# Joint tiles of the first batch placed ahead of the second batch's last conv unit and projection, with 25 seven-product groups in place of 21

## The chip, the cores and the metric

The kernel runs on one core of one Trainium2 chip. The metric is the device time of one execution in microseconds (us). The engines are named as the profile names them: PE is TensorE (the matrix engine), DVE is VectorE, ACT is ScalarE, POOL is GpSimd and SP is SyncE, which issues most transfers here.

## The reference

Two strided convolutions with gelu, a projection, and the joint network of a speech transducer. All inputs are bfloat16; B = 2, T = 4000, D = 512, K = 5 taps, U = 8.

```python
h = sum over i of xp[:, i:i+T, :] @ w1[i];   h = gelu(h)[:, ::2, :]      # 2000 rows a batch
f = sum over i of hp[:, i:i+T1, :] @ w2[i];  f = gelu(f)[:, ::2, :]      # 1000 rows a batch
fe = jnp.einsum("btd,de->bte", f, w_f)
ge = jnp.einsum("bud,de->bue", g, w_g)
j = jnp.tanh(fe[:, :, None, :] + ge[:, None, :, :])
return jnp.einsum("btud,dv->btuv", j, w_o)                               # (2, 1000, 8, 512)
```

The joint part is the largest: j has 2 x 8 x 1000 = 16000 rows of 512, each multiplied by the 512 x 512 matrix w_o.

## The kernel before

**Conv stages.** The first convolution is done in five tiles (a fast-filter form on TensorE, with combinations of inputs and weights made by DVE and ACT). The second, conv2, is computed with a form that yields three outputs per step: `Triple.unit(m, ...)` handles one batch b and one block m of 128 output channels. A unit consists of a first part (five products of four matmuls of 334 columns, then an ACT copy `cs` and five DVE scalar steps into `sd` and `acc`, and one gelu into `fT`) and of an end (four more products, t0, s0, ti and si, and two gelus), which is put on a list and emitted by `finish` one or two units later. `conv2(b, m)` in the changed kernel is the body of the old double loop. `fe(b)` is the projection by w_f: eight groups of four matmuls of 500 columns, half of them copied to `feT` by DVE and half by ACT.

**Joint stage.** The 16000 rows make 125 tiles of 128. `tanh(v, k)` is one ACT instruction: 128 channels (k of 4) of the 1000 rows of one (b, u) pair v (16 pairs), from feT[b] with a bias from ge, into `jT`, a ring of 3072 columns (split in two where the ring wraps). `tanhs(upto)` issues those that are needed up to a column, and a few ahead where the ring has room. A tile goes one of two ways:

- `Plain`: four matmuls of 512 columns into one bank of PSUM, one DVE eviction into `ost`, one store.
- `Seven`: four tiles at once as a 2 x 2 block product with seven multiplications instead of eight (Strassen's in Winograd's form). A product is four matmuls of 256 columns. `sums()` makes four combinations `ss` of jT: three on POOL, one on DVE (number 2). `wosums()` makes those of w_o, `tw`, once. The products accumulate in PSUM and are read out on the way: p1 is kept by ACT in an fp32 buffer `sn` (s1), p6 adds to the same bank and is kept (u2), p5 has its own bank and is kept (d5), and p2, p3 and p7 are each followed by a DVE add of a bank and a kept buffer into `og`, p4 by a plain eviction (DVE, or ACT in every fourth group). p3 adds to p5's bank, p7 and p4 to p1's, so each of p6, p3, p7 and p4 waits until the bank has been read. Four tiles are then stored from og.

Before, there are 21 groups and 41 plain tiles. The loop body for group q, with p the one before it and r its two plain tiles, is: p1(q), p7(p), p5(q), p2(q), first plain tile, sums of the next group, p6(q), p4(p), p3(q), second plain tile. fe(1) stands in the first iteration, behind p2.

**What sets the order.** Every operation is recorded with what it reads and writes, a cost and its place. From the point where `pl.pin = False`, a planner (`schedule`) lists operations onto the engines by estimated times: DVE and ACT take, of what is ready, the one with the least slack; TensorE, POOL and SP take the earliest recorded. The result is one static list per engine, with semaphore waits for what crosses engines. An engine works its list in order: an instruction that waits holds up all behind it.

Of the kernel before, what the change touches and what calls it, by code (L numbers as in the profile page):

```python
# [10 lines left out]
FP16 = mybir.dt.float16  # L11
FP32 = mybir.dt.float32
P = 128
# [260 lines left out]
def bass_standalone__seq2seq_rnn_t_joint__speech_kernel(  # L274
# [19 lines left out]
    B, T, D = x.shape  # L294
    K = w1.shape[0]
    U = g.shape[1]
    NK = D // P
    assert (B, T, D, K, U) == (2, 4000, 512, 5, 8)
    T1, T2 = T // 2, T // 4
# [5 lines left out]
    RING = 3072  # L305
    BU = B * U
    NT = 512
# [3 lines left out]
    with ExitStack() as es:  # L311
        cur = [16512]

        def at(name, shape, dtype, offset=None):
            o = cur[0] if offset is None else offset
            b = Buf(nc, name, shape, dtype, o)
            if offset is None:
                cur[0] = (b.end + 31) // 32 * 32
            return b

        xs = [at(f"xs{i}", [4, NK, XW], BF16) for i in range(3)]
# [3 lines left out]
        xt_off = cur[0]  # L325
        xt = [at(f"xt{i}", [4, NK, NT], BF16) for i in range(2)]
# [5 lines left out]
        hT = [at(f"hT{b}", [6, NK, HWID], BF16) for b in range(B)]  # L332
# [3 lines left out]
        ty = [at(f"ty{i}", [2, 256], FP32) for i in range(3)]  # L336
# [14 lines left out]
        assert row[0].bytes <= xt[0].bytes  # L351
        jT = at("jT", [NK, RING], BF16, w1_off)
        fT = [at("fT0", [NK, T2], BF16, jT.end), at("fT1", [NK, T2], BF16, xt_off)]
        feT = [at(f"feT{b}", [NK, T2], FP32, xs[2 * b].end - xs[2 * b].bytes) for b in range(B)]
        og = [at(f"og{i}", [4, NT], BF16, h_off + i * 4096) for i in range(3)]
        ost = [at(f"ost{i}", [NT], BF16, h_off + 12288 + i * 1024) for i in range(3)]
        assert fT[0].end <= xt_off and ost[-1].end <= h_off + hT[0].bytes
        h1 = hT[1].end - hT[1].bytes
        sn = [at(f"sn{i}", [NT], FP32, h1 + i * 2048) for i in range(7)]
        assert sn[-1].end <= hT[1].end  # L360
        ss = [at(f"ss{i}", [4, 2, NT // 2], FP16, xs[1].end - xs[1].bytes + i * 4096) for i in range(4)]
        assert ss[-1].end <= xs[1].end
        tw = at("tw", [4, 2, NT // 2], FP16, wg_sb.end - wg_sb.bytes)
        assert tw.end <= wg_sb.end
        ps = Psum(es.enter_context(nc.psum_tensor("acc", [P, 8 * NT], FP32)))
# [4 lines left out]
        def vec_cost(o, ins, fast=True):  # L370
            bf = fast and all(not v.psum and v.ap.dtype == BF16 for v in (o,) + tuple(ins))
            return o.ap.free_size() * (0.52e-3 if bf else 1.04e-3) + 0.065
# [3 lines left out]

        def tt(eng, o, a, b, op):
            pl.op(eng, lambda e: e.tensor_tensor(out=o.ap, in0=a.ap, in1=b.ap, op=op), (a, b), (o,),  # L378
                  0.15 + 2.2e-3 * o.ap.free_size() if eng == "pool" else vec_cost(o, (a, b)))

        def act(o, i, func, scale=1.0, bias=None):
            rd = (i,) if bias is None else (i, bias)
# [176 lines left out]
        def finish(keep=0):  # L559
            while len(ends) > keep:  # L560
                ends.pop(0)()
# [300 lines left out]
        def fe(b):  # L862
            for half in range(2):
                for m in range(NK):
                    v = ps.cols(bank(), NP2)
                    sl = slice(half * NP2, (half + 1) * NP2)
                    mm(v, [(wf_sb[k, m * P:(m + 1) * P], fT[b][k, sl]) for k in range(NK)], True, True)
                    o = feT[b][m, sl]
                    if m % 2:
                        act(o, v, ACT.Copy)  # L870
                    else:
                        pl.op("dve", lambda e, o=o, v=v: e.tensor_copy(out=o.ap, in_=v.ap), (v,), (o,), vec_cost(o, (v,)))  # L872

        def tanh(v, k):

            b, u = v // U, v % U
            lo, hi = v * T2, (v + 1) * T2
            while lo < hi:
                n = min(hi - lo, RING - lo % RING)
                t = lo - v * T2  # L880
                act(jT[k, lo % RING:lo % RING + n], feT[b][k, t:t + n], ACT.Tanh,
                    bias=geT[k * BU + v:k * BU + v + 1])
                lo += n
# [9 lines left out]
        def tail_zero(b):  # L893
            v = hT[b][2:6, :, HOFF + NT3 - 1:HOFF + NT3]
            memset(v)
# [9 lines left out]
        for qi in range(1, len(tiles)):  # L905
            tile = tiles[qi]
            nx = tiles[qi + 1] if qi + 1 < len(tiles) else None
            for m in range(WHOLE if qi == 1 else 0, NK):
# [12 lines left out]
                    tail_zero(0)  # L921
                if qi == 4 and m == 1:
                    ge()
        for b in range(B):
            for m in range(NK):
                steps, mid = LATE[b, m], ()
                if (b, m) == (0, 0):
                    mid = [lambda: finish(1), lambda: tail_zero(1)]
                if (b, m) == (1, 1):
                    mid = [lambda: fe(0)]  # L930
                trip[b].unit(m, [lambda b=b, w=w: trip[b].step(w) for b, w in steps], mid)
                if b == 1 and m in (2, 3):
                    for k in (2 * m - 4, 2 * m - 3):
                        tanh(0, k)


        ntile = B * U * T2 // P
        sems = {}
# [50 lines left out]
        class Seven:  # L989
# [4 lines left out]
            def __init__(self, jt):  # L994
                self.jt, self.n = jt, Seven.count
                Seven.count += 1
                self.c = jt * P % RING
                assert self.c + NT <= RING
                self.S = ss[self.n % len(ss)]
                self.o = og[self.n % len(og)]  # L1000

            def a(self, r, k):
                return jT[2 * k:2 * k + 2, self.c + r * H:self.c + (r + 1) * H]

            def sums(self):
                S = self.S
# [5 lines left out]

            def product(self, i, bk, start, check=False):

                lhs = {1: lambda t, k: jT[k, self.c + t * P:self.c + (t + 1) * P],
                       2: lambda t, k: jT[2 + k, self.c + t * P:self.c + (t + 1) * P],
                       4: lambda t, k: jT[2 + k, self.c + H + t * P:self.c + H + (t + 1) * P]}.get(i)
                if lhs is None:
                    si = {5: 0, 6: 1, 7: 2, 3: 3}[i]
                    lhs = lambda t, k: self.S[si, k, t * P:(t + 1) * P]  # L1020
                rhs = {1: lambda k: wo_sb[k, 0:H], 2: lambda k: wo_sb[2 + k, 0:H], 3: lambda k: wo_sb[2 + k, H:NT]}.get(i)
                if rhs is None:
                    ti = {5: 0, 6: 1, 7: 2, 4: 3}[i]
                    rhs = lambda k: tw[ti, k]
                for t in range(2):
                    mm(ps.cols(bk * NT + t * H, H), [(lhs(t, k), rhs(k)) for k in range(2)], start and t == 0, True, False)
# [29 lines left out]
            def p5(self):  # L1056
                self.D = take()
                self.product(5, self.D, True)
                self.d5 = self.keep("act", self.D)

            def p2(self):
                bk = take()
# [26 lines left out]
        def tanhs(upto, spread=None):  # L1089

            while state[0] < B * U and not pend and state[0] * T2 < upto + 900:
                pend.extend((state[0], k) for k in range(NK))
                state[0] += 1
            while pend and (pend[0][0] * T2 < upto or spread):
                v = pend[0][0]
                fits = (v + 1) * T2 - RING <= state[1] or (v + 1) * T2 <= RING
                if v * T2 >= upto and not fits:
                    break
                assert fits
                tanh(*pend.pop(0))  # L1100
                spread = None
                if not pend and state[0] < B * U and state[0] * T2 < upto:
                    pend.extend((state[0], k) for k in range(NK))
                    state[0] += 1

        plain = [Plain(0), Plain(1)]
        seven = [Seven(2 + 6 * i) for i in range(20)] + [Seven(121)]
        rest = [[Plain(6 * i + 6), Plain(6 * i + 7)] for i in range(18)] + [[Plain(n)] for n in (114, 115, 120)]
        wosums()
        tanhs(2 * P)  # L1110
        plain[0].go()
        plain[1].go()
        finish()
        tanhs(seven[0].jt * P + NT)
        seven[0].sums()
        for i, (q, r) in enumerate(zip(seven, rest)):
            p = seven[i - 1] if i else None
            state[1] = (p or q).jt * P
            base = q.jt * P
            if i + 1 < len(seven):  # L1120
                tanhs(seven[i + 1].jt * P + NT)
            else:
                tanhs(ntile * P)
            q.p1()
            if p:
                p.p7()
            q.p5()
            q.p2()
            if i == 0:
                fe(1)  # L1130
            if i + 1 < len(seven):
                r[0].go()
            if i + 1 < len(seven):
                seven[i + 1].sums()
            tanhs(base, True)
            q.p6()
            if p:
                p.p4()
            q.p3()
            if len(r) == 2:  # L1140
                r[1].go()
        seven[-1].p7()
        rest[-1][0].go(True)
        seven[-1].p4(True)

        pl.emit(block, [(s[0], s[1]) for s in sems.values()])

# [27 lines left out]
```

## Time and profile before

| | us |
|---|---|
| three timed runs | 265.88, 304.03, 1554.93 (median 304.03) |
| profiled execution | 265.86 |
| its span, first to last instruction | 264.1 |
| TensorE busy, granted clock | 257.3, 1.00 |
| DVE, ACT, POOL busy | 209.9, 196.2, 80.1 |
| first joint product (p1 of group 0) starts | 154.82 |
| last matmul starts | 259.73 |
| DMA, mean over the span | 121 GB/s |

The costliest groups of the joint stage (from 134 us on), in the profile's form: the line and engine, out<-in, count, busy time and the mean of one.

| group | count | busy us | mean ns |
|---|---|---|---|
| ACT jT<-feT,geT 128x1000 (the uncut tanh) | 44 | 50.2 | 1198 |
| DVE og<-acc,sn 128x512 | 63 | 42.3 | 684 |
| ACT sn<-acc 128x512 | 63 | 39.6 | 677 |
| DVE ost<-acc 128x512 | 40 | 27.3 | 682 |
| POOL ss, three kinds | 63 | 73.6 | 1164 to 1180 |
| DVE ss<-jT 128x512 | 21 | 16.7 | 797 |
| DVE og<-acc (p4's eviction) | 15 | 10.3 | 685 |

A duration counts from start to end of one instruction. Instructions of one engine overlap (the next starts before the last one's result is out), so the rate is read from the distance of two starts. A line of the timeline such as "188.86 1.46 PE ... x8" gives the start, the length and how many instructions were merged into it; "[0.18 <-PE acc]" behind a line is the idle time before it and what ended that.

### The profile page before, as it was taken

The page shows a single profiled execution, that of the slowest core. Times are in us where ns is not written, and L with a number is a line of the kernel's source. Part 1 is how long each engine was busy: PE and PEld are TensorE (multiplying, and loading weights), DVE is VectorE, ACT ScalarE, POOL GpSimd, SP SyncE. Part 2 cuts the span into 40 slices and gives each one's busy share as a digit, 9 for nine tenths or more (in the row PEclk, how much of TensorE's full clock was granted, in tenths as well). Part 3 has the DMA queues.
Part 4 walks back from the last instruction along what each step waited for, and adds up shares of the span by engine and source line. Part 5 has one row for each costly group of instructions (what it writes and reads, how often), then busy time and mean ns, then how long its engine had stood idle before and what let it go on. Part 6 is the DMA issues. An engine that isn't in the chain of part 4 may idle for free.

```text
span 264.1 us, 4770 instructions
## 1 busy us (share of the span) xinstructions
PE 257.3 (97%) x1738; PEld 167.3 (63%) x1738; DVE 209.9 (79%) x320; ACT 196.2 (74%) x269; POOL 80.1 (30%) x85
## 2 busy tenths in 40 slices
PE   8899999999999999999999999999999999999993
PEld 4797954444444445566646665777777777777782
DVE  1898999929999996299663744789899899889993
ACT  2637989348348723685679993898999999999942
POOL 1000000000000710000000974055785886929760
PEclk9999999999999999999999999999999999999999
DMA  6999999997000000000000000354454554645555
GB/s 246 301 178 196 201 211 217 191 352 224 2 0 0 0 2 0 0 2 1 0 2 0 20 24 0 126 167 159 155 185 142 170 180 139 207 144 171 168 181 172
DMA packets 54725, 31.92 MB, mean 121 GB/s; under 512 B 31646, under 2 KB 54446, under 8 KB 54702
## 3 DMA queue, kind: packets, MB, share of 16 engines
q1 hardware_dynamic: 54558, 31.55, 44.6%
q8 instruction: 14, 0.23, 0.4%
q14 instruction: 9, 0.07, 0.1%
q10 hardware_dynamic: 144, 0.07, 0.1%
HBM read 7.86 MB, written 16.38 MB: 92 GB/s over the span
## 4 chain that ended last, share of the span: by engine, by line
PE 88%; ACT 8%; DVE 1%; issue 1%; ACTq 0%
PE acc L391 88%; ACT jT L383 4%; ACT fT L383 2%; DVE xs L466 0%; ACT cs L383 0%; ACT xt L383 0%; ACT feT L383 0%; DVE xt L378 0%; DVE feT L872 0%; ACT og L383 0%; ACT hT L383 0%; PE acc L459 0%; ACTq L965 0%; ACT ost L383 0%; DVE zero L398 0%
## 5 line engine op out<-in xcount | busy, mean ns | idle before, releaser
L383 ACT ACTIVATE jT<-feT,geT 128x1000 bf16<-128x1000 f32 (+10 forms) x84 | 78.4, 1012 | 2.4 <-PE acc L391 1.4
L391 PE MATMUL acc<-wo_sb,jT 128*128 128x512 bf16 (+1 forms) x336 | 61.3, 323 | 0.0
L378 DVE TENSOR_TENSOR og<-acc,sn 128x512 bf16<-128x512 f32 x63 | 42.3, 684 | 9.9 <-ACT sn L383 7.4
L391 PE MATMUL acc<-xt,w_sb 128*128 128x252 bf16 (+2 forms) x240 | 45.9, 333 | 0.3 <-ACT hT L383 0.3
L378 POOL TENSOR_TENSOR ss<-jT 128x512 f16<-128x512 bf16 x21 | 24.4, 1164 | 71.5 <-PE acc L391 49.5
L391 PEld LDWEIGHTS acc<-wo_sb,jT 128*128 128x128 bf16 x336 | 32.9, 98 | 16.5
L383 ACT ACTIVATE sn<-acc 128x512 f32<-128x512 f32 x63 | 39.6, 677 | 4.3 <-PE acc L391 4.1
L391 PE MATMUL acc<-tw,ss 128*128 128x256 f16 x252 | 34.7, 273 | 0.0
L391 PEld LDWEIGHTS acc<-xt,w_sb 128*128 128x128 bf16 x240 | 23.3, 98 | 17.9 <-DVE ty L533 0.5
L955 DVE CAST ost<-acc 128x512 bf16<-128x512 f32 (+1 forms) x41 | 27.7, 676 | 2.4 <-PE acc L391 2.1
L391 PE MATMUL acc<-xs,w_t 128*128 128x498 bf16 (+2 forms) x140 | 29.5, 341 | 0.0
L391 PEld LDWEIGHTS acc<-tw,ss 128*128 128x128 f16 x252 | 24.6, 98 | 7.2
L383 ACT ACTIVATE hT<-acc 128x996 bf16<-128x996 f32 (+2 forms) x13 | 12.6, 968 | 21.0 <-PE acc L391 21.0
L378 POOL TENSOR_TENSOR ss<-jT,ss 128x512 f16<-128x512 bf16 x21 | 24.7, 1180 | 0.7
L378 POOL TENSOR_TENSOR ss<-ss,jT 128x512 f16<-128x512 f16 x21 | 24.5, 1169 | 0.7
L383 ACT ACTIVATE xt<-xs 128x1992 bf16<-128x1992 bf16 (+2 forms) x14 | 21.6, 1576 | 2.6 <-DMA xs<-in_x_dram 2.6
L391 PEld LDWEIGHTS acc<-xs,w_t 128*128 128x128 bf16 x140 | 13.5, 98 | 10.9 <-issue 0.3
L391 PE MATMUL acc<-xs,w_sb 128*128 128x252 bf16 (+2 forms) x104 | 19.3, 318 | 1.2 <-DVE xt L378 1.2
L378 DVE TENSOR_TENSOR ss<-jT 128x512 f16<-128x512 bf16 x21 | 16.7, 797 | 4.2 <-PE acc L391 2.2
L378 DVE TENSOR_TENSOR xt<-xt,xs 128x1992 bf16<-128x1992 bf16 (+2 forms) x14 | 14.2, 1012 | 5.7 <-ACT xt L383 5.7
L533 DVE SCALAR_TENSOR_TENSOR sd<-acc,cs 128x334 f32<-128x334 f32 x16 | 7.4, 499 | 12.9 <-PE acc L391 12.4
L391 PE MATMUL acc<-row,w_sb 128*128 128x334 bf16 x96 | 17.5, 305 | 0.0
(71 smaller groups left out, 363.3 us busy)
## 6 DMA issues: line engine op xcount, KB each, us to landing
out_dram<-og SPq DMA_DIRECT2D x75, 128.0 KB, 2.0
w_sb<-in_w_dram SPq DMA_DIRECT2D x10, 512.0 KB, 5.6
out_dram<-ost SPq DMA_DIRECT2D x34, 128.0 KB, 2.0
xr<-in_x_dram SPq DMA_DIRECT2D x2, 512.0 KB, 3.6
wg_sb<-in_w_g_dram SPq DMA_DIRECT2D x1, 512.0 KB, 8.8
wf_sb<-in_w_f_dram SPq DMA_DIRECT2D x1, 512.0 KB, 7.0
wo_sb<-in_w_o_dram SPq DMA_DIRECT2D x1, 512.0 KB, 7.9
xs<-in_x_dram SPq DMA_TRANSPOSE x16, 5.6
```

The source lines that it names most:

```text
L378: pl.op(eng, lambda e: e.tensor_tensor(out=o.ap, in0=a.ap, in1=b.ap, op=op), (a, b), (o,), 0.15 + 2.2e-3 * o.ap.free_size() if eng == "poo ...
L383: pl.op("act", lambda e: e.activation(o.ap, i.ap, func, scale=scale, bias=0.0 if bias is None else bias.ap), rd, (o,), o.ap.free_size() * ...
L391: ins = e.matmul(o.ap, lhsT=l.ap, rhs=r.ap, start=start and n == 0, stop=stop and n == len(pairs) - 1, skip_group_check=not check)
L533: pl.op(eng, lambda e: e.scalar_tensor_tensor(out=o.ap, in0=a.ap, scalar=f, in1=b.ap, op0=ALU.mult, op1=add), (a, b), (o,), vec_cost(o, (a ...
L955: pl.op("dve", lambda e: e.tensor_copy(out=o.ap, in_=v.ap), (v,), (o,), vec_cost(o, (v,)))
```

## The change

The diff, with lines that only move buffers' assertions cut:

```diff
-        feT = [at(f"feT{b}", [NK, T2], FP32, xs[2 * b].end - xs[2 * b].bytes) for b in range(B)]
+        feT = [at("feT0", [NK, T2], FP32, xs[0].end - xs[0].bytes), at("feT1", [NK, T2], FP32, xt[1].end - xt[1].bytes)]
...
-        h1 = hT[1].end - hT[1].bytes
-        sn = [at(f"sn{i}", [NT], FP32, h1 + i * 2048) for i in range(7)]
-        ss = [at(f"ss{i}", [4, 2, NT // 2], FP16, xs[1].end - xs[1].bytes + i * 4096) for i in range(4)]
+        homes = [xt_off + 8192 + i * 2048 for i in range(4)] + [y.end - y.bytes for y in ty]
+        sn = [at(f"sn{i}", [NT], FP32, o) for i, o in enumerate(homes)]
+        ss = [at(f"ss{i}", [4, 2, NT // 2], FP16, xs[2].end - xs[2].bytes + i * 4096) for i in range(4)]
...
-                  0.15 + 2.2e-3 * o.ap.free_size() if eng == "pool" else vec_cost(o, (a, b)))
+                  0.02 + 2.14e-3 * o.ap.free_size() if eng == "pool" else vec_cost(o, (a, b)))
...
-        for b in range(B):
-            for m in range(NK):
...
-                trip[b].unit(m, [lambda b=b, w=w: trip[b].step(w) for b, w in steps], mid)
-                if b == 1 and m in (2, 3):
-                    for k in (2 * m - 4, 2 * m - 3):
-                        tanh(0, k)
+        def conv2(b, m):
...
+            trip[b].unit(m, [lambda b=b, w=w: trip[b].step(w) for b, w in steps], mid)
+
+        for m in range(NK):
+            conv2(0, m)
+        for m in range(2):
+            conv2(1, m)
...
-                self.c = jt * P % RING
+                self.c = [(jt + 2 * r) * P % RING for r in range(2)]
...
-                self.d5 = self.keep("act", self.D)
+                self.d5 = self.keep("dve" if self.n < 15 else "act", self.D)
...
-        plain = [Plain(0), Plain(1)]
-        seven = [Seven(2 + 6 * i) for i in range(20)] + [Seven(121)]
-        rest = [[Plain(6 * i + 6), Plain(6 * i + 7)] for i in range(18)] + [[Plain(n)] for n in (114, 115, 120)]
+        seven = [Seven(2 + 4 * i) for i in range(15)] + [Seven(62 + 6 * i) for i in range(10)]
+        rest = [[] for _ in range(15)] + [[Plain(66 + 6 * i), Plain(67 + 6 * i)] for i in range(10)]
+        hooks = {4: lambda: conv2(1, 3), 5: finish, 9: lambda: fe(1)}
         wosums()
-        tanhs(2 * P)
-        plain[0].go()
-        plain[1].go()
+        for k in range(NK):
+            tanh(0, k)
+        conv2(1, 2)
         finish()
-        tanhs(seven[0].jt * P + NT)
+        Plain(0).go()
+        Plain(1).go()
...
-            if i == 0:
-                fe(1)
...
+            if i in hooks:
+                hooks[i]()
         seven[-1].p7()
-        rest[-1][0].go(True)
+        Plain(122).go()
         seven[-1].p4(True)
+        Plain(123).go()
+        Plain(124).go(True)
```

In words: the groups become 25 and the plain tiles 25. Groups 0 to 14 cover tiles 2 to 61 (almost all of the first batch's 62.5) with no plain tile between them; groups 15 to 24 have two plain tiles each, as before; tiles 122 to 124 are plain and come last. The second batch's conv2 units 0 and 1 stay ahead of the joint stage, unit 2 is recorded after the first four tanh, unit 3 behind group 4, its end behind group 5, and fe(1) behind group 9. The keeping of d5 goes from ACT to DVE in groups 0 to 14. A group's four tiles may now lie across the ring's end (two pairs with addresses of their own). sn, ss and feT1 lie in other memory: sn over the end of xt0 and the three ty, ss over xs2, feT1 over xt1. The planner's cost for a POOL operation on 512 columns falls from 1.28 to 1.12.

More of the change, by code (lines that the diff above doesn't have):

```diff
@@ L353, in bass_standalone__seq2seq_rnn_t_joint__speech_kernel @@
         fT = [at("fT0", [NK, T2], BF16, jT.end), at("fT1", [NK, T2], BF16, xt_off)]
-        feT = [at(f"feT{b}", [NK, T2], FP32, xs[2 * b].end - xs[2 * b].bytes) for b in range(B)]
+        feT = [at("feT0", [NK, T2], FP32, xs[0].end - xs[0].bytes), at("feT1", [NK, T2], FP32, xt[1].end - xt[1].bytes)]
+        assert feT[1].end <= xt[1].end and fT[1].end <= xt_off + 8192
         og = [at(f"og{i}", [4, NT], BF16, h_off + i * 4096) for i in range(3)]
@@ L357, in bass_standalone__seq2seq_rnn_t_joint__speech_kernel @@
         assert fT[0].end <= xt_off and ost[-1].end <= h_off + hT[0].bytes
-        h1 = hT[1].end - hT[1].bytes
-        sn = [at(f"sn{i}", [NT], FP32, h1 + i * 2048) for i in range(7)]
-        assert sn[-1].end <= hT[1].end
-        ss = [at(f"ss{i}", [4, 2, NT // 2], FP16, xs[1].end - xs[1].bytes + i * 4096) for i in range(4)]
-        assert ss[-1].end <= xs[1].end
+        homes = [xt_off + 8192 + i * 2048 for i in range(4)] + [y.end - y.bytes for y in ty]
+        sn = [at(f"sn{i}", [NT], FP32, o) for i, o in enumerate(homes)]
+        assert sn[3].end <= xt[0].end
+        ss = [at(f"ss{i}", [4, 2, NT // 2], FP16, xs[2].end - xs[2].bytes + i * 4096) for i in range(4)]
+        assert ss[-1].end <= xs[2].end
         tw = at("tw", [4, 2, NT // 2], FP16, wg_sb.end - wg_sb.bytes)
@@ L923, in bass_standalone__seq2seq_rnn_t_joint__speech_kernel @@
                     ge()
-        for b in range(B):
-            for m in range(NK):
[L926 to L930, printed above, removed]
-                trip[b].unit(m, [lambda b=b, w=w: trip[b].step(w) for b, w in steps], mid)
-                if b == 1 and m in (2, 3):
-                    for k in (2 * m - 4, 2 * m - 3):
-                        tanh(0, k)
+        def conv2(b, m):
+            steps, mid = LATE[b, m], ()
+            if (b, m) == (0, 0):
+                mid = [lambda: finish(1), lambda: tail_zero(1)]
+            if (b, m) == (1, 1):
+                mid = [lambda: fe(0)]
+            trip[b].unit(m, [lambda b=b, w=w: trip[b].step(w) for b, w in steps], mid)
[3 more added lines that the diff above has]
+            conv2(1, m)
         ntile = B * U * T2 // P
@@ L996, in __init__ @@
                 Seven.count += 1
-                self.c = jt * P % RING
-                assert self.c + NT <= RING
+                assert jt % 2 == 0 and RING % (2 * P) == 0
+                self.c = [(jt + 2 * r) * P % RING for r in range(2)]
                 self.S = ss[self.n % len(ss)]
@@ L1002, in a @@
             def a(self, r, k):
-                return jT[2 * k:2 * k + 2, self.c + r * H:self.c + (r + 1) * H]
+                return jT[2 * k:2 * k + 2, self.c[r]:self.c[r] + H]
             def sums(self):
@@ L1013, in product @@
             def product(self, i, bk, start, check=False):
-                lhs = {1: lambda t, k: jT[k, self.c + t * P:self.c + (t + 1) * P],
-                       2: lambda t, k: jT[2 + k, self.c + t * P:self.c + (t + 1) * P],
-                       4: lambda t, k: jT[2 + k, self.c + H + t * P:self.c + H + (t + 1) * P]}.get(i)
+                tile = lambda r, t, k: jT[k, self.c[r] + t * P:self.c[r] + (t + 1) * P]
+                lhs = {1: lambda t, k: tile(0, t, k), 2: lambda t, k: tile(0, t, 2 + k),
+                       4: lambda t, k: tile(1, t, 2 + k)}.get(i)
                 if lhs is None:
@@ L1119, in bass_standalone__seq2seq_rnn_t_joint__speech_kernel @@
             base = q.jt * P
[L1120 to L1123, printed above, removed]
+            last = i + 1 == len(seven)
+            tanhs(ntile * P if last else seven[i + 1].jt * P + NT)
             q.p1()
@@ L1128, in bass_standalone__seq2seq_rnn_t_joint__speech_kernel @@
             q.p2()
-            if i == 0:
-                fe(1)
-            if i + 1 < len(seven):
+            if r:
                 r[0].go()
-            if i + 1 < len(seven):
+            if not last:
                 seven[i + 1].sums()
@@ L1139, in bass_standalone__seq2seq_rnn_t_joint__speech_kernel @@
             q.p3()
-            if len(r) == 2:
+            if r:
                 r[1].go()
+            if i in hooks:
+                hooks[i]()
         seven[-1].p7()
-        rest[-1][0].go(True)
+        Plain(122).go()
         seven[-1].p4(True)
+        Plain(123).go()
+        Plain(124).go(True)
         pl.emit(block, [(s[0], s[1]) for s in sems.values()])
```

## The prediction

> **What bounds the kernel now.** I read the page's busy lines first, then the chain that ended last, then the timeline of the joint stage engine by engine, since the change lies there.
>
> ```profile
> PE 257.3 (97%) x1738; PEld 167.3 (63%) x1738; DVE 209.9 (79%) x320; ACT 196.2 (74%) x269; POOL 80.1 (30%) x85
> ...
> PE   8899999999999999999999999999999999999993
> ...
> DVE  1898999929999996299663744789899899889993
> ACT  2637989348348723685679993898999999999942
> POOL 1000000000000710000000974055785886929760
> ```
>
> TensorE (PE) is busy nearly throughout. In the right third, the joint stage, VectorE (DVE) and ScalarE (ACT) stand at 8 to 9 tenths beside it: there is little room to load them more.
>
> ```profile
> 22.61 113.38 PE acc L391 x664
> ...
> 136.72 1.13 ACT jT L383
> ...
> 156.45 103.06 PE acc L391 x764
> ```
>
> The chain of waits follows TensorE from 22.61 to 136 and again from 156.45 to 259.5; between, it walks through ACT, but TensorE's starts in the timeline show no hole there (104 conv matmuls and two plain tiles from 138.33 to 154.82: 104 x 0.1415 + 8 x 0.217 = 16.4 us, all of it). So the bound is TensorE's issue rate, and the next thing to see is that rate, and how near the others are.
>
> ```profile
> 188.86 1.46 PE L391 MATMUL acc<-wo_sb,jT 128*128 128x512 bf16 x8
> ...
> 190.16 1.04 PE L391 MATMUL acc<-tw,ss 128*128 128x256 f16 x8
> ...
> 190.28 0.68 DVE L378 TENSOR_TENSOR og<-acc,sn 128x512 bf16<-128x512 f32 x1
> ...
> 190.88 0.67 DVE L955 CAST ost<-acc 128x512 bf16<-128x512 f32 x1
> ...
> 191.03 1.46 PE L391 MATMUL acc<-wo_sb,jT 128*128 128x256 bf16 x8
> ...
> 191.47 1.27 DVE L378 TENSOR_TENSOR og<-acc,sn 128x512 bf16<-128x512 f32 x2
> ...
> 193.64 1.46 PE L391 MATMUL acc<-wo_sb,jT 128*128 128x512 bf16 x8
> ```
>
> Starts tell the rate, durations include the pipeline. Eight 256-column matmuls take 191.03 - 190.16 = 0.87, so one of the seven products (4 matmuls) is 0.434 us and a group 3.04. From 188.86 to 193.64 is one iteration (a group and two plain tiles): 4.78 = 3.04 + 8 x 0.217, gapless. DVE's starts on 512 columns are 0.60 apart. By the same reading ACT's evictions into sn are 0.48 apart (188.86 to 189.34).
>
> ```profile
> 140.04 3.17 ACT L383 ACTIVATE jT<-feT,geT 128x1000 bf16<-128x1000 f32 x3
> ...
> 143.09 0.73 ACT L383 ACTIVATE fT<-acc 128x334 bf16<-128x334 f32 x1
> ...
> 143.61 0.77 ACT L383 ACTIVATE fT<-sd 128x333 bf16<-128x333 f32 x1
> ```
>
> A tanh is 1.02 (three from 140.04 to 143.09), a gelu into fT 0.54.
>
> ```profile
> 203.34 0.41 DVE L378 TENSOR_TENSOR ss<-jT 128x512 f16<-128x512 bf16 x1
> 203.67 0.68 DVE L955 CAST og<-acc 128x512 bf16<-128x512 f32 x1
> ...
> 208.24 1.15 POOL L378 TENSOR_TENSOR ss<-jT 128x512 f16<-128x512 bf16 x1
> 208.38 1.29 DVE L378 TENSOR_TENSOR ss<-jT 128x512 f16<-128x512 bf16 x1 [0.70 <-ACT jT L383]
> ...
> 209.35 1.34 POOL L378 TENSOR_TENSOR ss<-jT,ss 128x512 f16<-128x512 bf16 x1
> 209.59 0.68 DVE L378 TENSOR_TENSOR og<-acc,sn 128x512 bf16<-128x512 f32 x1
> ```
>
> DVE's own sum takes a slot of 0.33 while GpSimd (POOL) rests (203.34 to 203.67), but 1.21 when it starts inside a POOL sum (208.38 to 209.59). POOL's sums are 1.11 apart (208.24 to 209.35), and the one that follows a held-up DVE sum is longer, 1.34.
>
> **What the change saves.** Four more groups take the place of 16 plain tiles: 4 x (4 x 4 x 0.217 - 3.04) = 1.73 us of TensorE. The wait of fe(1)'s first matmul goes: it starts at 156.45, where the product before it, begun at 155.69, leaves TensorE free at 156.12, so 0.3. In its new place fe(1) comes some 15 us after its last gelu, and next late there would be a bank, which group 9's DVE adds free before that. At the end, the last work is now half a plain tile, evicted in 256 columns (0.38 in the row at 259.53) with one store, where p4's 512 columns (0.60) and two stores stood: about 0.4. p4 still follows p7 by 0.87 us of plain matmuls, so its wait of 0.23 stays. Together 2.4: all hidden costs aside, 265.86 - 2.4 = 263.5.
>
> **What it costs.** Fifteen groups now run without plain tiles between. In such a bare group TensorE needs 3.04. DVE needs three og adds, the d5 copy that moves to it from ACT for the first 15 groups, and p4's cast in three of four: 4.75 x 0.60 = 2.85, plus its sum, 0.33 to 1.2. Ten sums from 189.00 to 248.18 met a POOL sum; their slots (start to next start) add up to 9.48, a mean of 0.95. That is 3.18 to 3.80 a group: more than TensorE's 3.04. POOL needs 3 x 1.12 = 3.36 and up to 0.33 lost to DVE's sum. ACT needs 2.25 x 0.48 plus 512/1000 x 4 x 1.02 of tanh: 3.17. All three are over TensorE's time. With two plain tiles in between, as before, DVE needed 5.7 x 0.60 and a sum, 3.8 to 4.4, ACT 3.3 x 0.48 + 0.768 x 4 x 1.02 = 4.7, POOL 3.4, all under TensorE's 4.77. The moved work covers part of it: conv2(1,3) (20 matmuls behind group 4, 16 behind group 5, 36 x 0.1415 = 5.1 on TensorE, 5 x 0.46 on DVE) and fe(1) behind group 9 (6.75 on TensorE, 4 x 0.60 on DVE). Neither issues a DMA, and the same tiles are stored, by groups instead of plain tiles.
>
> I followed the static instruction lists of the changed kernel by hand with these slots. **Start:** ACT's list puts ten tanh, seven gelus, a cs and two feT copies between 136.72 and its first sn: 10.2 + 3.8 + 0.33 + 0.94 = 15.3, so that sn starts at 152.0. TensorE has conv2(1,2) and three ends, 68 x 0.1415 = 9.6 from 138.2, two plain tiles, p1, p5, p2 and half of the next p1: 151.1. p6 must wait for the sn, 152.6: 1.5 lost, where before fe(1) stood there as cover. DVE's list has the sum of group 3, whose tanh comes at 151.9, ahead of the first d5; behind it are p3 and all of DVE's later evictions: 0.5 more. **Groups 1 to 4:** two DVE sums (0.7 to 1.1 each in a POOL stretch) delay og(1,1) and d5, and p4 and p3 accumulate into the banks these free: waits of 0.5, 0.1, 0.2 and 0.8, so 1.6. **Behind group 5:** DVE makes two sums under conv2(1,3), so its scalar steps end late and the conv end waits 0.7. **Groups 6 to 8:** 0.4, one sum. **Groups 10 to 14:** three sums less a cast that is ACT's: 0.6, part of which group 15's plain tiles cover. Sum 2.0 + 1.6 + 0.7 + 0.4 + 0.6 = 5.3. The bounds: nothing, if buffers absorb each delay, to 0.76 (3.80 - 3.04) on each of the 12 bare groups without cover, 9.1, with the start's 2.0 and the conv end's 0.7: 11.8. I take the replay by hand between them, because the lists place half of the sums under the two covers.
>
> At no cost: the moved buffers (sn over xt and ty, ss in xs2, feT1 in xt1) wait only for conv work that ended long before, and the sums may start some 3 us earlier than at 145.45, as the tanh come; if not, p5 of group 0 still has its first POOL sum, 1.16 long, by 147. Stores: 4 of 128 KB per 3.04 us, against 6 per 4.78, with the same 0.5 DMA share; SP's issues of 0.4 to 0.55 fill 2.2 of 3.04. ACT after fe(1): 38 evictions x 0.48 and 35 of tanh, 53 us from about 197, ends near 250, and the last group begins 8.2 us (3.04 + 1.73 + 3.5 of tail) before TensorE's end of some 263: 4 us to spare. The POOL constant changes the planner's order only, which the lists above hold.
>
> The row at 208.38 bears on the order of these sums. The Trainium skill, "SBUF — State Buffer", section "Who interferes with whom", says that a VectorE instruction with two SBUF inputs and a GpSimd instruction reading SBUF exclude one another, the later one being blocked for the whole of the other. Both rows agree with it; taken strictly, every DVE sum in unbroken POOL work would be blocked, and by the rule alone the time would be that of the second rival below.
>
> **The numbers.** The sum stands on the profiled execution: span 264.1, 1.76 around it, 265.86, which is the lowest of the three timed runs (265.88; their median is 304.03, the highest 1554.93), so mine is for an undisturbed execution: 265.86 - 2.4 + 5.3 = 268.8.
>
> **Forecast** (chance 0.55): within 2%, slightly slower, own range 265.5 to 271.5. **Rival one, all hidden** (0.15): the eight banks and seven sn buffers absorb the delays; 263.5 to 265. For it: DVE's sum can fall to 0.33, then a bare group needs 3.18, and the fillers cover that. Against: ACT's start at 152.0. **Rival two, starved** (0.27), the slower side: DVE's sum meets POOL in every bare group, each group takes 3.80, and 265.86 - 2.4 + 11.8 = 275.3; it decides from a mean loss of 0.4 per bare group on (12 x 0.4 + 2.7 = 7.5 gives 271.0; the 2% line is 271.2). For it: POOL alone would need 3.36. **Rival three, not what it says** (0.03): the moved conv tail changes the order of the conv stage too. The lists up to conv2(1,2) are the same on TensorE, which speaks against it; it would have to find over 5 us where TensorE has no hole.
>
> 2% is about what a measurement here can tell from no change. Faster by that: 0.04 (rival three and an unseen cover). Slower: 0.24 of rival two and 0.04 of the forecast, 0.28. Within: 0.68. The range takes rival one whole and stops inside rival two: 263.3 to 273.
>
> **What would show it.** TensorE's starts from 150: a hole of about 1.5 us before group 0's p6, released by ACT's sn; then holes under 1 us at p3 and p4, released by DVE og and sn. DVE's sums at 0.9 or more while POOL runs. fe(1) without a wait. Plain stretch at 4.77 per iteration. I am wrong if the bare groups run at 3.04 from group 1 on, or if holes come from POOL.

## The result, and the profile after

The changed kernel takes 270.53 us (median of four runs, 270.38 to 270.83), against 265.88 before: a ratio of 1.0174 with a 95% interval of 1.015 to 1.0199. So it is slower, by less than 2% but by far more than the interval's width. The time lies inside the predicted range (263.3 to 273.0) and 1.7 above the forecast of 268.8. The ratio leaves out the 304.03 and 1554.93 of the table of before, which are disturbed runs. The profiled execution took 270.83, its span is 269.0.

The page's busy lines, engine by engine, and the span in 40 slices (each digit is tenths busy):

```profile
PE 257.9 (96%) x1786; PEld 170.3 (63%) x1786; DVE 223.2 (83%) x338; ACT 195.4 (73%) x267; POOL 94.9 (35%) x97
...
PE   8799999999999999999999799899999999999992
...
DVE  1899999929999993499637599999989998889872
```

TensorE still looks full, with a 7 where the joint stage begins (the slice from 148 us) and an 8 in the slice from 168 us, and DVE stands at 8 or 9 from 155 us nearly to the end. Busy tenths don't show where 4.9 us of span went; TensorE's starts do. From its timeline (start, length, work, matmuls merged, and in brackets the idle time and what ended it):

```profile
148.11 2.32 PE L392 MATMUL acc<-wo_sb,jT 128*128 128x512 bf16 x12
...
150.71 0.82 PE L392 MATMUL acc<-wo_sb,jT 128*128 128x256 bf16 x6
152.63 0.61 PE L392 MATMUL acc<-tw,ss 128*128 128x256 f16 x4 [1.10 <-ACT sn L384]
...
154.00 0.61 PE L392 MATMUL acc<-wo_sb,ss 128*128 128x256 bf16 x4 [0.32 <-DVE sn L956]
...
172.59 0.39 PE L392 MATMUL acc<-tw,jT 128*128 128x256 f16 x2 [0.75 <-DVE og L379]
```

A row's own slots are its length less 0.164 (one 256-column matmul is 0.273 long and takes a slot of 0.109). So six matmuls from 150.71 free TensorE at 151.37, and p6 of group 0 starts at 152.63: a hole of 1.26. Read like this for every row from 136 us on, gaps over 0.03 added up, the holes are 5.26 us, against 0.73 before. Each large one is at p6, p3 or p4, and is ended by ACT's sn, or by DVE's sn or og; none is ended by POOL. In the groups with plain tiles, an iteration is 4.79 (plain tiles start at 216.12 and at 220.91 in the same view), as before.

The first hole as ACT has it (ACT's rows of the timeline):

```profile
150.44 0.76 ACT L384 ACTIVATE fT<-acc 128x333 bf16<-128x333 f32 x1
150.95 1.14 ACT L384 ACTIVATE jT<-feT,geT 128x1000 bf16<-128x1000 f32 x1
151.94 0.63 ACT L384 ACTIVATE sn<-acc 128x512 f32<-128x512 f32 x1
```

ACT does not rest ahead of this sn. The twelve matmuls from 148.11 are the first two plain tiles and p1 of group 0, so p1's last matmul starts at about 150.2; but a gelu and a tanh stand ahead of its sn in ACT's list, and the sn starts at 151.94. And the largest hole behind that, 0.92 before p4 at 172.59, as DVE has it:

```profile
168.68 2.42 DVE L379 TENSOR_TENSOR ss<-jT 128x512 f16<-128x512 bf16 x2
171.03 0.91 DVE L534 SCALAR_TENSOR_TENSOR sd<-acc,cs 128x334 f32<-128x334 f32 x2
171.85 0.67 DVE L379 TENSOR_TENSOR og<-acc,sn 128x512 bf16<-128x512 f32 x1
```

Two sums of 1.2 each and two scalar steps of conv2(1,3) stand ahead of the og add that frees p4's bank.

The end of the kernel changed most against expectation. The chain that ended last (start, us, step):

```profile
262.00 2.02 DMA out_dram<-ost
...
264.05 0.69 DVE ost L956
```

And the timeline of the last 8 us, all engines:

```profile
262.00 3.12 SPq L966 DMA_DIRECT2D out_dram<-ost  x2
...
264.05 0.69 DVE L956 CAST ost<-acc 128x512 bf16<-128x512 f32 x1 [0.22 <-DMA out_dram<-ost]
...
265.16 0.93 SPq L966 DMA_DIRECT2D out_dram<-og  x2
266.13 0.95 SPq L966 DMA_DIRECT2D out_dram<-ost  x2
```

TensorE's last slot ends at 263.64, yet the span ends at 269.0: a tail of 5.36, against 3.92 before. An eviction at 264.05 waits for a store issued at 262.00 to land, SP's second ost store (inside the 3.12) waits for that eviction, and four more stores stand behind it in SP's queue.

So the span's 269.0 - 264.1 = 4.9 is: holes +4.53 (5.26 - 0.73), tail +1.44, start of conv2(1,2) +0.13 (138.46 against 138.33), and TensorE's own slots -1.20.

### The profile page after: what moved, and what is told of

Read it like the earlier page. It is cut to its first block, busy times and chain, and to the rows that moved or that the text cites. A ratio compares the mean times of both kernels' runs of the same rounds, so it can differ in the third digit from the quotient of the medians.

```text
span 269.0 us, 4919 instructions
## 1 busy us (share of the span) xinstructions
PE 257.9 (96%) x1786; PEld 170.3 (63%) x1786; DVE 223.2 (83%) x338; ACT 195.4 (73%) x267; POOL 94.9 (35%) x97
## 5 line engine op out<-in xcount | busy, mean ns | idle before, releaser
L392 PE MATMUL acc<-wo_sb,jT 128*128 128x256 bf16 (+1 forms) x304 | 53.2, 306 | 0.0
L379 DVE TENSOR_TENSOR og<-acc,sn 128x512 bf16<-128x512 f32 x75 | 49.7, 679 | 4.2 <-PE acc L392 2.6
L379 POOL TENSOR_TENSOR ss<-jT 128x512 f16<-128x512 bf16 x25 | 29.1, 1176 | 55.1 <-ACT jT L384 52.9
L392 PE MATMUL acc<-tw,ss 128*128 128x256 f16 x300 | 41.4, 273 | 1.1 <-ACT sn L384 1.1
L384 ACT ACTIVATE sn<-acc 128x512 f32<-128x512 f32 x60 | 35.8, 607 | 6.5 <-PE acc L392 6.2
L392 PEld LDWEIGHTS acc<-tw,ss 128*128 128x128 f16 x300 | 29.0, 98 | 7.7 <-ACT sn L384 1.9
L379 POOL TENSOR_TENSOR ss<-ss,jT 128x512 f16<-128x512 f16 x25 | 29.6, 1195 | 0.8
L379 POOL TENSOR_TENSOR ss<-jT,ss 128x512 f16<-128x512 bf16 x25 | 29.4, 1188 | 0.8
L379 DVE TENSOR_TENSOR ss<-jT 128x512 f16<-128x512 bf16 x25 | 23.4, 944 | 2.8 <-ACT jT L384 2.8
L956 DVE CAST ost<-acc 128x512 bf16<-128x512 f32 (+1 forms) x25 | 16.9, 676 | 4.1 <-PE acc L392 3.6
```

What stands on the lines that cost most here:

```text
L384: pl.op("act", lambda e: e.activation(o.ap, i.ap, func, scale=scale, bias=0.0 if bias is None else bias.ap), rd, (o,), o.ap.free_size() * ...
L392: ins = e.matmul(o.ap, lhsT=l.ap, rhs=r.ap, start=start and n == 0, stop=stop and n == len(pairs) - 1, skip_group_check=not check)
L956: pl.op("dve", lambda e: e.tensor_copy(out=o.ap, in_=v.ap), (v,), (o,), vec_cost(o, (v,)))
```

## The experiments

All are edits of the changed kernel unless it is said otherwise. Times are medians, each ratio is against the kernel before on the same chip; holes, slots' end and tail are read from each run's own profile as above.

| kernel | us | ratio, 95% interval | span | holes | tail |
|---|---|---|---|---|---|
| before | 265.88 | | 264.1 | 0.73 | 3.92 |
| after | 270.53 | 1.0174 [1.015, 1.0199] | 269.0 | 5.26 | 5.36 |
| e1_ost_order | 268.88 | 1.0109 [1.0092, 1.0125] | 267.4 | 5.37 | 3.70 |
| e2_d5_act | 267.58 | 1.0057 [1.0038, 1.0076] | 265.1 | 2.54 | 5.36 |
| e3_no_dve_sum | 267.56 | 1.0056 [1.0039, 1.0074] | 266.2 | 2.60 | 5.41 |
| e4_conv3_first | 267.80 | 1.0067 [1.0049, 1.0084] | 265.4 | 2.94 | 5.35 |
| e5_conv_fe_first | 269.97 | 1.0151 [1.0136, 1.0166] | 267.9 | 4.68 | 5.35 |
| e6_21_groups | 266.44 | 1.0019 [1.0007, 1.0031] | 264.9 | 1.42 | 3.87 |
| e7_all_three | 265.72 | 0.9985 [0.9975, 0.9995] | 263.8 | 2.23 | 4.17 |
| e8_costs | 263.70 | 0.9911 [0.9889, 0.9933] | 261.9 | 0.28 | 3.76 |
| e9_gelu_cost | 265.30 | 0.9976 [0.9963, 0.999] | 263.6 | 2.06 | 3.74 |
| e10_sum_cost | 264.97 | 0.997 [0.9954, 0.9986] | 263.2 | 2.01 | 3.74 |
| e11_26_groups | 263.15 | 0.9897 [0.9882, 0.9912] | 261.4 | 0.14 | 3.82 |
| e12_before_costs | 265.54 | 0.9987 [0.9976, 0.9998] | 263.7 | 0.58 | 3.88 |

**The tail.** A `Plain` takes one of three ost buffers by a counter when it is constructed, not when it runs. After the change, the 20 plain tiles of `rest` are constructed before Plain(0) and Plain(1), and so tile 121 (number 19) and tile 122 (number 22), which run one behind the other, both get ost 1. The edit hands the buffers out in the order of running:

```diff
-                self.jt, self.s = jt, Plain.count % len(ost)
-                Plain.count += 1
+                self.jt = jt
...
-                r0, s = self.jt * P % RING, self.s
+                r0, s = self.jt * P % RING, Plain.count % len(ost)
+                Plain.count += 1
```

> The changed kernel with the three ost buffers handed out in the order in which the plain tiles run (tiles 121 and 122 no longer share one). Theory A (the tail was mis-sized: tile 122's eviction waits for the landing of tile 121's store out of the same buffer, and three stores queue behind it on SP): TensorE's part is unchanged, the time from its last matmul to the end falls from 5.4 to 3.4-3.9 us, so 268.5 to 269.0 us. Rival (the end is bound by the SP queue or the DMA engines whatever the buffer): 270.3 to 270.7.

Measured: 268.88, with the holes unchanged (5.37) and the tail 5.36 - 3.70 = 1.66 shorter; the time fell by 1.65. Its last us, in the timeline of all engines:

```profile
261.72 0.69 DVE L956 CAST ost<-acc 128x512 bf16<-128x512 f32 x1
...
263.64 0.81 SPq L966 DMA_DIRECT2D out_dram<-og  x2
...
264.13 0.42 DVE L956 CAST ost<-acc 128x256 bf16<-128x256 f32 x1 [0.86 <-DMA out_dram<-ost]
```

Tile 122 is now evicted at 261.72, and p4's stores leave at 263.64 in place of 265.16. A wait for a landing is left (0.86), but only the last tile's halves are behind it.

**DVE, ACT or POOL as the bound of the bare groups.** The first edit gives d5 of all groups back to ACT. The second leaves out DVE's sum in groups 0 to 14 (product 7 reads sum 0 there, so the output blocks that take product 7 hold other values in these groups):

```diff
-                self.d5 = self.keep("dve" if self.n < 15 else "act", self.D)
+                self.d5 = self.keep("act", self.D)
```

```diff
-                    tt(eng, S[i], x, y, op)
+                    if i != 2 or self.n >= 15:
+                        tt(eng, S[i], x, y, op)
...
-                    si = {5: 0, 6: 1, 7: 2, 3: 3}[i]
+                    si = {5: 0, 6: 1, 7: 2 if self.n >= 15 else 0, 3: 3}[i]
```

> The changed kernel with d5 kept by ACT in all 25 groups. 15 copies leave DVE (15 x 0.60 = 9.0 us) and join ACT (15 x 0.48 = 7.2). If DVE alone holds the bare groups: 267 to 269.5. If ACT is as near its limit as the sum says (2.25 x 0.48 + 2.09 + 0.48 = 3.65 per bare group against 3.04), the holes only change their owner: 270.5 to 275, with waits on ACT sn and jT in place of DVE.

> The changed kernel without DVE's sum in groups 0 to 14; their seventh product reads another sum instead, so one of four output blocks of these groups holds other values. Theory A (the DVE sum that waits for POOL's makes the holes of groups 1 to 14, 3.5 us by TensorE's starts): 267 to 268.5, the start's hole of 1.3 us before group 0's p6 stays, the one behind it falls. Rival (DVE's five other operations or ACT make them): at least 269.7.

Measured: 267.58 and 267.56, holes 2.54 and 2.60. Both take away about half, and both leave the first hole whole (1.25 and 1.26, ended by ACT's sn). So DVE's list holds TensorE up behind the start, and ACT, which takes 15 more evictions in the first edit, had room for them: its hole did not grow. So over this stretch with its covers ACT isn't the bound that the prediction's 3.17 against 3.04 for one bare group made of it.

**What the two covers do.** Conv unit (1,3) and its end ahead of the joint stage; and that with fe(1) back in the first iteration:

```diff
-        hooks = {4: lambda: conv2(1, 3), 5: finish, 9: lambda: fe(1)}
+        hooks = {9: lambda: fe(1)}
...
         conv2(1, 2)
+        conv2(1, 3)
         finish()
```

> The changed kernel with conv2(1,3) and its end right behind conv2(1,2), ahead of group 0; fe(1) stays behind group 9. Theory A: the 5.1 us of TensorE work cover ACT's lateness, so the start's holes (1.75 us) go; in return groups 4 to 8 lose the cover in which DVE caught up, and get 1 to 2.5 us of holes: 269.5 to 271.5. Rival (the start's wait is not ACT's arrears of tanh and gelu but a fixed cost of group 0): the start's hole stays at 1.2 or more and the time rises to 271 to 273.

```diff
+        hooks = {}
...
+        conv2(1, 3)
...
+            if i == 0:
+                fe(1)
```

> The changed kernel (25 groups, its tail, d5 on DVE) with conv2(1,3), its end and fe(1) at their old places: ahead of group 0, and inside group 0. Theory A: fe(1) covers ACT's lateness as before, so the start's holes (1.75 us) go; the bare groups 1 to 14 then have no cover at all, and DVE (3.18 to 3.80 against 3.04) costs 0.2 to 0.5 on each: 3 to 7 us of holes, 268.5 to 272.5. Rival (the bare groups need no cover, the moved conv work is what hurts): under 1.5 us of holes, 266 to 267.5.

Measured: 267.80 and 269.97. The first is a miss on the good side. The hole at the start shrinks from 1.26 + 0.48 to 0.42, as ACT's backlog of tanh and gelu then lies beside conv work; the holes that come in its place (0.67 at 175.52, 0.46 at 179.05, 0.43 at 207.64) are smaller than I had thought. A cover at the start was worth more than the one behind group 4. With both covers gone from the bare groups the start's hole is gone, but 4.68 of holes open elsewhere, far from any conv work (0.67 at 182.03 and 0.43 at 189.00, and 0.72 at 233.41, where the plain tiles are back).

**The move without the bare groups.** The old 21 groups, each with its two plain tiles, in the new place behind conv2(1,2) (conv2(1,3) behind group 3, its end behind group 4, fe(1) behind group 6, d5 on ACT):

```diff
-        seven = [Seven(2 + 4 * i) for i in range(15)] + [Seven(62 + 6 * i) for i in range(10)]
-        rest = [[] for _ in range(15)] + [[Plain(66 + 6 * i), Plain(67 + 6 * i)] for i in range(10)]
+        seven = [Seven(2 + 6 * i) for i in range(20)] + [Seven(121)]
+        rest = [[Plain(6 * i + 6), Plain(6 * i + 7)] for i in range(18)] + [[Plain(n)] for n in (114, 115, 120)]
```

> The old 21 groups, plain tiles and tail, all d5 on ACT, but with the first batch's joint tiles ahead of conv2(1,3) (behind group 3, its end behind group 4) and fe(1) (behind group 6). Theory A: only the start's hole is left (1.2 to 1.8 us before group 0's p6), fe(1)'s old wait of 0.3 goes, no holes in the groups: 266.6 to 267.6. Rival (moving the conv work costs more, by buffers or banks): 268 or more; other rival (nothing at the start either): 265.5 to 266.

Measured: 266.44, 0.2% above before, a little under what was expected. The start's hole is 0.56, where 1.2 to 1.8 was expected; one more is 0.37 (at 242.98, ended by ACT's sn), the last p4's wait is 0.39, as before, and the tail is the old one (3.87). So the move alone is nearly free, and 270.53 - 266.44 = 4.1 us come with the bare groups and the new end.

**Three repairs together**: e1, e2 and e4.

> The changed kernel with ost in running order, all d5 on ACT, and conv2(1,3) ahead of group 0. Theory A: the three gains add as far as they touch different holes: 1 to 2 us of holes, a tail of 3.7: 264.2 to 265.6, below the kernel before. Rival (ACT, with d5 and conv's gelus ahead, becomes late): 266 or more, with holes released by ACT.

Measured: 265.72, just above the band. The holes up to 204 us are 0.42 (at the start) and less, but one opened late:

```profile
237.82 1.02 PE L392 MATMUL acc<-wo_sb,jT 128*128 128x512 bf16 x4 [0.82 <-ACT jT L384]
```

TensorE's timeline shows a plain tile of the late groups waiting for a tanh: with d5 on ACT and the conv work ahead, ACT's tanh are late by 237 us. Neither e2 nor e4 alone has this hole. So moving load away from DVE is a cure with an end: in e7 the largest hole (0.98 by TensorE's starts) is ACT's.

**Load or order.** Two of the planner's costs don't fit the slots of the trace. A gelu into fT (333 or 334 columns) is charged 0.33, and takes 0.51 to 0.57 from start to next start (150.44 to 150.95 above is 0.51). DVE's sum is charged 0.60 and takes up to 1.2 beside POOL (two in 168.68 to 171.03). e8 corrects both and has e1's edit; work, instructions and their engines are the same as in after:

```diff
         def vec_cost(o, ins, fast=True):
+            if o.ap.dtype == FP16:
+                return 0.95
...
-                  o.ap.free_size() * 0.833e-3 + (0.05 if i.psum else 0.105 if bias is None else 0.186))
+                  0.54 if func == ACT.Gelu_apprx_tanh and o.ap.free_size() < 335 else
+                  o.ap.free_size() * 0.833e-3 + (0.05 if i.psum else 0.105 if bias is None else 0.186))
```

> The changed kernel with ost in running order and two costs of the planner set to the measured slots: 0.54 for a gelu into fT (planned 0.33) and 0.95 for DVE's sum (planned 0.60). No work is added or taken away; ACT's list then has group 0's first sn ahead of a tanh and a gelu, and DVE's has d5 ahead of group 3's sum. Theory B (the holes come from lists ordered by wrong slots): 1 to 2.5 us of holes instead of 5.3, 264.5 to 266.3. Theory A in its strict form (the load of a bare group is over TensorE's time, whatever the order): only the start's part and the tail change, 267 to 268.9.

Measured: 263.70, ratio 0.9911 [0.9889, 0.9933]: below the expected band, and faster than before. The holes fall from e1's 5.37 to 0.28, which is 5.1 of the 5.5 between the two spans; conv2(1,2) starts 0.25 earlier, and the rest lies in the slots and the tail. The page's busy lines of e8:

```profile
PE 255.8 (98%) x1786; PEld 171.3 (65%) x1786; DVE 219.1 (84%) x338; ACT 194.4 (74%) x267; POOL 95.2 (36%) x97
```

The counts are those of after. What moved shows first at the start (timeline of e8):

```profile
149.98 0.60 PE L395 MATMUL acc<-tw,ss 128*128 128x256 f16 x4
150.18 0.60 ACT L386 ACTIVATE sn<-acc 128x512 f32<-128x512 f32 x1
...
150.67 0.73 ACT L386 ACTIVATE fT<-acc 128x333 bf16<-128x333 f32 x1
...
150.85 0.60 PE L395 MATMUL acc<-tw,ss 128*128 128x256 f16 x4
```

The row at 149.98 is p5, and p1 stands right ahead of it. ACT now reads p1's bank at 150.18, ahead of the last gelu and a tanh, and p6 follows at 150.85 without a wait. Then at conv2(1,3) (DVE's rows of e8):

```profile
166.82 0.69 DVE L381 TENSOR_TENSOR ss<-jT 128x512 f16<-128x512 bf16 x1
167.43 0.90 DVE L537 SCALAR_TENSOR_TENSOR sd<-acc,cs 128x334 f32<-128x334 f32 x2
...
171.29 0.87 DVE L381 TENSOR_TENSOR ss<-jT 128x512 f16<-128x512 bf16 x1
172.08 0.68 DVE L381 TENSOR_TENSOR og<-acc,sn 128x512 bf16<-128x512 f32 x1
172.68 0.77 DVE L381 TENSOR_TENSOR ss<-jT 128x512 f16<-128x512 bf16 x1
```

One sum stands ahead of the scalar steps where after has two in a row, and the next two have an og add between them. They are also shorter. DVE's groups from 150 to 214 us, the bare stretch, in after (first) and e8 (second): count, busy time and mean ns of one sum.

```profile
L379 DVE TENSOR_TENSOR ss<-jT 128x512 f16<-128x512 bf16 x13 | 14.9, 1161 | 1.4 <-ACT jT L384 1.4
```

```profile
L381 DVE TENSOR_TENSOR ss<-jT 128x512 f16<-128x512 bf16 x14 | 11.6, 829 | 0.4 <-ACT jT L386 0.4
```

So the order also sets the load: a sum is 0.33 shorter on average, by where it falls beside POOL's.

The two costs one by one, each with e1's edit:

> As the kernel with ost in running order and both planner costs set to the measured slots (263.7 us), but with the gelu's cost alone (0.54); DVE's sum is planned at 0.60 again. If the gelu's cost does it all (ACT's list at the start, and what the late start hands on to DVE): 263.3 to 264.3, under 0.8 us of holes. If the sum's cost is needed for the holes of groups 1 to 14: the start's 1.75 go, up to 3.5 stay: 265 to 267.

> The same with the DVE sum's cost alone (0.95); the gelu is planned at 0.33 again, so ACT's list at the start is the changed kernel's. If the two costs each remove their own part: the start's 1.26 before p6 and 0.5 behind it stay, the rest goes: 265 to 266. If the later holes follow from the late start: 267 to 268.9, as with ost in running order alone.

Measured: 265.30, in its band, and 264.97, just below its own; holes 2.06 and 2.01. With the gelu's cost alone the 1.26 at the start is gone, the 0.92 at group 4 too, while 0.36 at p3 and the 0.41 and 0.45 at groups 10 to 14 stay (197.94 and 207.45). With the sum's cost alone the 1.26 stays to the hundredth, and those behind it go but one (0.41). The start's hole is therefore the gelu's cost, the late ones are the sum's; the 0.92 goes by either.

**More bare groups, and the costs without the change.** e11 is e8 with 26 groups, 18 of them bare (d5 stays with DVE in the first 15 alone):

```diff
-        seven = [Seven(2 + 4 * i) for i in range(15)] + [Seven(62 + 6 * i) for i in range(10)]
-        rest = [[] for _ in range(15)] + [[Plain(66 + 6 * i), Plain(67 + 6 * i)] for i in range(10)]
+        seven = [Seven(2 + 4 * i) for i in range(18)] + [Seven(74 + 6 * i) for i in range(8)]
+        rest = [[] for _ in range(18)] + [[Plain(78 + 6 * i), Plain(79 + 6 * i)] for i in range(8)]
```

> The 263.7 us kernel (ost in running order, both costs measured) with 26 groups, the first 18 of them bare, and 21 plain tiles. Four tiles more in a group save 4 x 4 x 0.217 - 3.04 = 0.43 us of TensorE. Theory B (order, not load, made the holes; there is room left): 263.0 to 263.6. Theory A (a bare group's load is over TensorE's time, so three more bare groups after fe(1) cost 0.2 to 0.76 each): 264 to 265.8.

e12 is the kernel before with the two costs and nothing else.

> The kernel before, with the two planner costs set to the measured slots and nothing else. TensorE has 0.7 us of holes there, so little can be won: 265.0 to 266.2 by both theories. 264.5 or less would say that the costs gain something apart from the change.

Measured: 263.15, ratio 0.9897 [0.9882, 0.9912], holes 0.14, the lowest time of the study; and 265.54, ratio 0.9987. One more group was to bring 4 x 4 x 0.217 - 3.04 = 0.43; e8 to e11 is 0.55, but the intervals of the two overlap. The holes did not grow, so three bare groups more did not bring a bound into sight. Without the change the costs are worth 0.1%: the gain of e8 isn't the costs' own but the change's, which they let through.

## Why the prediction was right in its range and wrong in the tail and in its reason

**The saving on TensorE** (1.73): the slots (from conv2(1,2)'s start to the last slot's end, less holes) are 1.20 shorter in after and 1.42 in e8. Part of the rest is a rounded slot: in the kernel before, matmul starts without a hole between them are on average 0.1092 apart at 256 columns and 0.2158 at 512, so a group is 28 x 0.1092 = 3.06, not 3.04, and four groups save 4 x (16 x 0.2158 - 28 x 0.1092) = 1.58. What is left, 0.16 to 0.38, may lie in gaps below 0.03, which are not counted as holes.

**The wait of fe(1)** (0.3): right. It has no wait in its new place. **The last p4's wait** (to stay): wrong, and in the change's favour. Two plain tiles, 1.73 in place of 0.87, stand between the last p7 (260.16) and p4 (262.33) in TensorE's list, and the hole of 0.40 before p4 is gone.

**The tail** (predicted 0.4 shorter; measured 1.44 longer): this step failed. I costed the last tile's matmuls, eviction and stores, and took for granted that the stores of the tiles ahead of it were no matter. Two things were missed, both readable beforehand: which ost buffer each of the last plain tiles has, and what stands in SP's queue behind a store that has to wait. The step is off by 1.84. That 268.8 + 1.84 = 270.6 meets the time is luck in part: the slots saved 0.53 less than forecast and conv2(1,2) started 0.13 later, while the holes grew by 4.53 in place of 5.3 - 0.3 = 5.0, and these three nearly cancel. e1 shows the tail's cause: with other buffers and nothing else, 1.65 of it goes. Against the predicted end 0.2 remains; a wait for a landing is left at the last tile there, but no run shows that it is this 0.2.

**The start** (2.0): measured 1.26 + 0.48 = 1.74, at p6 and p3, released by ACT's sn and DVE's sn, as promised. **Groups 1 to 4** (1.6): 0.8. **Around group 5** (0.7): 1.0, but the 0.92 is at group 4's p4 behind the sums and the scalar steps, where I had put it at the conv end. **Groups 6 to 8** (0.4): 0.4. **Groups 10 to 14** (0.6): 1.2. With 0.1 at 245.38 that is 5.26 for 5.3; the sum is better than its terms, since their errors cancel.

**The reason** given for the 5.3, that a bare group asks more than 3.04 of DVE, ACT and POOL alike, failed for ACT and POOL, and for DVE it is not what the work brings with it. No hole is ended by POOL; e2 gave ACT 15 evictions more and TensorE's one large wait for it did not grow; and e8 has the same instructions on the same engines and 0.28 of holes. The balance has to be made over the whole bare stretch with its covers, not over one group. TensorE has 15 x 3.04 + 5.1 + 6.75 = 57.5 us there. DVE has 15 x 2.85 + 2.3 + 2.4 = 47.5 of other work, less than TensorE, and 15 sums. At the mean lengths of the stretch less 0.07 of overlap these are 16.4 in after and 11.4 in e8: 63.9 or 58.9. In after DVE is over TensorE by 6.4, of which holes of 4.0 show (5.26 less the start's 1.26, which is ACT's); in e8 by 1.4 us over 15 groups, and a sum can be made early or late, as there are four sets of ss. So the order decides both how long the sums take and whom they hold up. The planner made that order with slots that are too short, 0.60 and 0.33, and put sums and gelus ahead of the short work that frees banks. My replay took the lists as they were, with the right slots, and so came to the right size, 5.3; it then explained by load what the lists had done.

**The rivals.** Starved (275.3, a mean loss of 0.76 in every bare group) fell: groups 6 to 8 lose about 0.4 in all. All hidden (263.5 to 265) fell for the kernel as it is, yet its arguments were the better ones on what the engines allow: e8's 263.70 is inside its band. That the change does not do what it says fell.

**The rule on VectorE and GpSimd.** The Trainium skill, "SBUF — State Buffer", section "Who interferes with whom", has a VectorE instruction with two SBUF inputs and a GpSimd instruction that reads SBUF contend for a shared port that one of them holds exclusively. The sums fit it (0.41 long at best, as at 212.98 in after, 1.2 and more beside POOL), and taking 15 of them away (e3) took 2.7 us of holes away. Used as a price for every group it would have given the starved rival, and no run came near that: a sum has to meet POOL, and the list decides whether it does, with whom behind it.

**The signs** came as promised: a hole of 1.26 for the 1.5 before p6, then holes under 1 us at p3 and p4 by DVE, sums of 1.16 on average in the bare stretch, fe(1) without a wait, 4.79 per plain iteration. No sign had been named for the tail, since it was thought settled.

**What stays open.** Why the slots show 1.2 to 1.4 of a saving of 1.58; and which single moves of the order in e8 matter, beyond the two shown. The 0.95 for the sum was one value, and no other was tried, nor was the order changed by costs that fit the trace no better; so it isn't shown how much of the gain needs costs that are right.

## What to carry to other kernels

When tiles are moved to the end of a kernel, write down for the last half dozen which store buffer each has, whose landing that buffer waits for, and what stands in the store queue behind it; here that was 1.65 us. Where a planner orders the work, compare each of its costs with the distance of starts in the trace before a change brings the engines closer together: two wrong costs were worth 0.1% in a kernel with slack, and 1.9% (268.88 to 263.70) in one without. And an engine whose summed work is near the bound is not yet the bound: separate what can be made early from what frees a bank.

## What the runs showed of the hardware that was not expected

A gelu of 333 or 334 PSUM columns into fT, written with a stride of three elements, takes 0.51 to 0.56 of ACT, where a copy of 334 columns (cs at 139.83, next start 140.16 in after) takes 0.33. The runs don't tell the function from the stride. The start of conv2(1,2), with the same work ahead of it, was anywhere from 137.33 to 138.46 in these profiles; 1.1 us of one profiled span against another is therefore no evidence of the edit, which is why the holes and tails are compared here and not the spans alone.
